# Retention attention and a top-2 expert layer: queries in 1-KB rows, later weight loads, and five expert tiles inside the last routing

## The chip, the cores and the metric

The kernel runs on one core of one Trainium2 chip. The metric is the device time of one execution in microseconds; the comparison is between the medians of repeated executions of the kernel before and the kernel after. Engines are named as in the profile: PE is TensorE's matmul, PEld its weight load, DVE VectorE, ACT ScalarE, POOL GpSimd, SP the queue that issues most DMAs.

## What is computed

```python
# q, k, v: (8 batches, 8 heads, 576 positions, 64)
scores = q @ k.T / 8
ret = scores * gamma[h] ** (i - j)     # where i >= j, else 0; gamma = 1 - 2**(-5-h)
x = (ret @ v)                          # as rows of 512: 4608 tokens (8 heads x 64)

logits = x @ w_gate + log1p(exp(x @ w_noise)) * noise       # 8 experts
top2, weights = two largest, softmax over the two
out = sum over the two experts e of  weight * (relu(x @ w1[e]) @ w2[e])   # 512 -> 1024 -> 512
```

## The kernel before, in words

**Attention.** Each batch's 576 positions are 512 plus a tail of 64. A *unit* is one batch and four heads (16 units); units 4b to 4b+3 make a pair of batches (`bp`), 1152 tokens. `Attention.load(u)` brings in a unit's q, k and v, two DMAs of 256 KB each per tensor: a partition holds two adjacent tokens of a head, so a row of a DMA is 2 x 64 x 4 = 512 bytes. `cast` makes bf16 copies: keys and values on POOL, queries on ACT. `tr` transposes queries or keys on PE, `scores` makes the scores of half a unit (mask on DVE), `states` the running sums of key times value (copied out on ACT), `out` the unit's output (decay on DVE, into `xT`). The `*_tail` functions do the 64-position tails of a pair.

**Routing.** `Router.route(bp)` is a Python generator that routes the 1152 tokens of a pair in 18 pieces. It computes the gate matmuls (L383), the logits `lg` (L388), the two best experts on DVE, the rank of each token in its expert's list with a matmul (L470, L472) over running counts `cum`, and writes the tokens with their gate values as rows of 1056 bytes to a DRAM table `xd` (L531). At the end a matmul of two one-hot tables (L551) adds the tokens' row numbers to the lists `L` (L555). `finish` turns `L` into the list of row numbers `xi` (three DVE instructions, L564 to L567), and `overflow_list` works out tiles for tokens beyond the lists' capacity (here there are none in the profile).

First choices (the lower-numbered expert of a token's two) fill an expert's list from the front, second choices from the back. Each list has 1280 slots, five tiles of 256 tokens.

**The order of work.** Rounds n = 0 to 16 of the main loop issue the parts of unit n and n-1. Seven times a round `step()` advances the pending routing by one piece. Under `manual_schedule` the order in which instructions are written is their order on each engine. A routing is put in the pending list near the end of rounds 4, 8, 12 and 16; the last one has no attention work beside it and runs out in `while pend: step()`. Weights of experts 0 and 1 are loaded by POOL-queue DMAs with a cast (L924, L927) after rounds 5, 7, 9 and 11.

**Experts.** `experts` loops over 40 tiles (8 experts x 5). For tile i: `gather` (an indirect DMA by `xi`, two halves of 128 rows), `transp` (8 transposes), `g1` (32 matmuls of 128x256, relu on ACT or DVE), `g2` (16 matmuls of 128x512). `g2` of a tile is interleaved with `g1` of the next. First choices' results go to a DRAM table `yd`; for second choices the first result is gathered back (`prev`), added (`comb`) and scattered to the output (`scat`). Weights of experts 2 to 7 are loaded through staging buffers and cast on ACT during the loop (`wload`, `wcast`). 11 DVE memsets (L717, L719) clear the gather buffers; they are outside the hand-written order.

Of the kernel before, what the change touches and what calls it, by code (L numbers as in the profile page):

```python
# [9 lines left out]
F32 = mybir.dt.float32  # L10
# [23 lines left out]
NOV = 80  # L34
# [4 lines left out]
CAPB = [P * (HPE - n) for n in ONLYA]  # L39
ROW0 = [P + sum(CAPA[:e]) for e in range(E + 1)]  # L40
# [5 lines left out]
def constants(nc, cp):  # L46
# [21 lines left out]
    for h in range(2):  # L68
        for rs in range(2):
            m = K["mask"][h * HD:(h + 1) * HD, rs, :].rearrange("p (r q) -> p r q", r=2)  # L70
            nc.gpsimd.affine_select(m, m, pattern=[[1, 2], [2, HD]], base=-rs, channel_multiplier=-2,
                                    compare_op=Alu.is_ge, fill=0.0)
# [8 lines left out]
    K["tok"] = cp.tile([P, 4, NC9], F32, name="tok")  # L81
    for h in range(2):
        t = K["tok"][h * HD:(h + 1) * HD]
        for b in range(2):
            nc.gpsimd.iota(t[:, :, 4 * b:4 * b + 4], pattern=[[1152, 4], [P, 4]], base=h + 576 * b,
                           channel_multiplier=2, allow_small_or_imprecise_dtypes=True)
# [13 lines left out]
def decay_tables(nc, cp, tmp):  # L100
# [5 lines left out]
    nc.gpsimd.iota(tv[:, :512].rearrange("p (c r q) -> p c r q", c=4, r=2), pattern=[[P, 4], [1, 2], [2, HD]],  # L106
# [20 lines left out]
class Attention:  # L127


    def __init__(self, tc, ctx, K, q, k, v):  # L130
# [5 lines left out]
        self.raw = ep("at_raw", 4)  # L136
# [21 lines left out]
    def load(self, u, queues):  # L158
        bp, hq, b = self.unit(u)
        d = self.u[u] = {}  # L160
        for n, q in zip("qkv", queues):
            r = self.raw.tile([P, 2, 4, P], F32, name=f"raw_{n}")
            for c in range(2):
                q.dma_start(out=r[:, c], in_=self.src[n][2 * bp + b, 4 * hq:4 * hq + 4, 256 * c:256 * c + 256, :].rearrange(  # L164
                    "h (p r) d -> p h (r d)", r=2))
            d["raw" + n] = r
# [9 lines left out]
    def cast(self, u):  # L176
# [6 lines left out]
        for r in range(2):  # L183
# [8 lines left out]
        qb = self.bf.tile([P, 2, 2, 4, HD], BF16, name="qb")  # L192
        nc.scalar.activation(qb.rearrange("p r c h d -> p (c h) r d"),
                             d.pop("rawq").rearrange("p c h (r d) -> p (c h) r d", r=2), Act.Copy, scale=0.125)
# [29 lines left out]
    def tr(self, u, n):  # L224
# [5 lines left out]
        for hp in range(2):  # L230
            for c in range(2):
                for r in range(2):
                    nc.tensor.transpose(p[:, hp, c, r, :], src[:, r, c, 2 * hp:2 * hp + 2, :].rearrange(
                        "p h d -> p (h d)"), self.K["ident"])
# [3 lines left out]
        d[n.upper()] = t  # L238

    def scores(self, u, hp):  # L240
# [3 lines left out]
        for c in range(2):  # L244
            for r in range(2):
                for h in range(2):
                    s = slice(h * HD, (h + 1) * HD)
                    for e in range(2):
                        nc.tensor.matmul(p[h][e * HD:(e + 1) * HD, c, r, :].rearrange("p (r q) -> p r q", r=2),  # L249
                                         lhsT=d["K"][s, hp, c, r, e, :], rhs=d["Q"][s, hp, c, :, e, :],  # L250
# [30 lines left out]
    def out(self, u):  # L281
# [17 lines left out]
        for e in range(2):  # L299
            for hp in range(2):  # L300
                for c in range(2):
                    j = 2 * c + e
                    if j:
                        nc.tensor.matmul(p[e][:, hp, c, :].rearrange("p (r q) -> p r q", r=2),
                                         lhsT=d["T", hp][:, j - 1, :], rhs=d["Q"][:, hp, c, :, e, :], start=False,
# [32 lines left out]

class Router:
# [13 lines left out]

    def load_noise(self, j):
# [3 lines left out]
        nq = nm[:, :512, :].rearrange("b (c q r) e -> q r b c e", q=HD, r=2)  # L358
        nt = nm[:, 512:, :].rearrange("(p b) s e -> s b p e", b=2)
        for c in range(4):  # L360
            nc.sync.dma_start(out=self.noise[j * HD:(j + 1) * HD, :, c, :], in_=nq[:, j, :, c, :])
        nc.sync.dma_start(out=self.noiset[j * HD:(j + 1) * HD], in_=nt[:, j])

    def route(self, bp):
# [112 lines left out]
        V.tensor_mul(pd, M, pr)  # L477
# [3 lines left out]
        V.tensor_copy(prs, pr[:, :, 0])  # L481
        V.tensor_add(prs, prs, pr[:, :, 1])
# [73 lines left out]
        else:  # L556
            V.tensor_copy(self.L, pT)

# [10 lines left out]
    def overflow_list(self):  # L569
# [4 lines left out]
        pn = self.at.ps.tile([P, 2, E], F32, name="R", bufs=1)  # L574
        nc.tensor.matmul(pn.rearrange("p a e -> p (a e)"), lhsT=self.K["ones"],
                         rhs=self.cum[:, NCOL].rearrange("p a e -> p (a e)"), start=True, stop=True)
# [3 lines left out]
        V.tensor_copy(ct, pn[:, 0])  # L580
        V.tensor_add(ct, ct, pn[:, 1])
# [484 lines left out]
```

## Time and profile before

| | |
|---|---|
| timed runs | 625.11, 619.98, 621.22 us; median 621.22 us |
| profiled execution | 616.24 us, of which the span in the trace is 614.7 us |
| mean granted TensorE clock | 0.821 of full speed |
| busy in the span | PE 460.4 us (75%), PEld 318.8 (52%), DVE 288.5 (47%), ACT 259.4 (42%), POOL 269.1 (44%) |
| moved by DMA | 104.19 MB, 170 GB/s on average |

The page cuts the span into 40 slices of 15.4 us. A digit is the busy share of a slice in tenths; the row PEclk gives the clock that TensorE was granted, in tenths. In rows of the order of time the first two numbers are start and duration in us, and a bracket at the end holds the idle time of the engine before that instruction with what ended it. "issue" is idle time in which the engine waited for nothing that the profile shows. A matmul's duration includes its passage through the array, so matmuls overlap: their spacing, not their duration, is the rate.

### The profile page before, as it was taken

To read this page: it belongs to the slowest core of one execution; us is meant where nothing else is said; L and a number is where in the kernel's file an instruction comes from. 1 tells how busy PE (TensorE), PEld (TensorE's weight loads), DVE (VectorE), ACT (ScalarE), POOL (GpSimd) and SP (SyncE) were. 2 spreads that over 40 slices of the span, in tenths; PEclk is the share of its full clock that TensorE was granted. 3 is DMA by queue.
4 is the path that set the end of the run, shared out by engine and by line. 5 is a ranking of instruction groups with operands and counts; after the bars stand their busy time and mean duration, and the time that the engine had idled before them with its cause. 6 is when DMAs were issued, how large, how long until landed. Compare 5 with 4: busy or idle time off the path is not lost.

```text
span 614.7 us, 11772 instructions
## 1 busy us (share of the span) xinstructions
PE 460.4 (75%) x4625; PEld 318.8 (52%) x4625; DVE 288.5 (47%) x783; ACT 259.4 (42%) x366; POOL 269.1 (44%) x339
## 2 busy tenths in 40 slices
PE   0688648828746334699999799899799598899960
PEld 0466536627634223466667356566466365565640
DVE  0266896798788775133333134234143243344440
ACT  6557625724641311165465154364354351332200
POOL 9644544337031037621303702705616447656560
PEclk9987557656676555889999979989989799989995
DMA  9997999969102322265666645665765554434450
GB/s 224 270 245 173 227 283 268 251 126 225 29 2 81 136 80 76 79 188 190 190 216 208 204 158 197 208 207 173 232 201 189 199 166 132 152 119 132 135 185 24
DMA packets 104491, 104.19 MB, mean 170 GB/s; under 512 B 25575, under 2 KB 81385, under 8 KB 104432
## 3 DMA queue, kind: packets, MB, share of 16 engines
q1 hardware_dynamic: 87088, 69.51, 39.3%
q0 software_dynamic: 15232, 32.84, 19.9%
q10 hardware_dynamic: 2112, 1.05, 0.7%
q8 instruction: 37, 0.61, 0.4%
q14 instruction: 22, 0.18, 0.1%
HBM read 84.66 MB, written 28.72 MB: 184 GB/s over the span
## 4 chain that ended last, share of the span: by engine, by line
PE 30%; issue 25%; DVE 19%; POOL 7%; DMA 6%; ACT 4%; SPq 4%; another core or an unknown queue 2%; POOLq 0%; ACTq 0%; DVEq 0%
PE p L807 11%; PE po L826 10%; POOL xg L758 4%; DVE S L254 3%; PE T L270 2%; SPq L164 2%; DVE olo L535 2%; SPq L172 2%; PE R L551 2%; DVE xT L310 2%; POOL prv L834 2%; DMA xg<-xd,xi 1%; DMA prv<-yd,ix 1%; POOL out_dram L868 1%
## 5 line engine op out<-in xcount | busy, mean ns | idle before, releaser
L807 PE MATMUL p<-xgT,w 128*128 128x256 bf16 x1280 | 254.4, 283 | 20.9 <-issue 20.3
L826 PE MATMUL po<-w,hT 128*128 128x512 bf16 x640 | 249.0, 393 | 6.7 <-issue 4.4
L807 PEld LDWEIGHTS <-w 128*128 128x128 bf16 x1280 | 129.1, 101 | 115.9 <-issue 40.0
L814 DVE TENSOR_SCALAR hT<-p 128x512 bf16<-128x512 f32 x80 | 55.2, 691 | 224.9 <-PE p L807 150.8
L812 ACT ACTIVATE hT<-p 128x512 bf16<-128x512 f32 x80 | 47.8, 597 | 198.8 <-PE p L807 91.4
L758 POOL DMA_INDIRECT xg<-xd,xi x80 | 81.4, 1018 | 44.3 <-issue 21.4
L868 POOL DMA_INDIRECT out_dram<-o,ix x45 | 45.6, 1014 | 124.5 <-DVE o L862 116.9
L826 PEld LDWEIGHTS <-hT 128*128 128x128 bf16 x640 | 64.2, 100 | 19.9 <-issue 10.2
L834 POOL DMA_INDIRECT prv<-yd,ix x45 | 45.6, 1014 | 32.3 <-DMA wst<-in_moe_w_dram 18.9
L254 DVE TENSOR_TENSOR S<-S,mask 128x512 bf16<-128x512 f32 x64 | 41.1, 684 | 37.5 <-PE S L249 37.5
L794 ACT ACTIVATE xgT<-pt 128x1024 bf16<-128x1024 bf16 x40 | 40.8, 1019 | 21.3 <-PE pt L791 18.3
L754 ACT ACTIVATE w<-wst 128x1024 bf16<-128x1024 f32 x48 | 47.9, 1048 | 0.0
L437 POOL TENSOR_TENSOR cum<-cum,M 128x16 bf16<-128x16 bf16 x36 | 8.0, 222 | 64.8 <-DVE d L442 62.3
L791 PE MATMUL pt<-ident,xg 128*128 128x128 bf16 x320 | 27.0, 225 | 12.5 <-issue 4.6
L276 ACT ACTIVATE Tb<-T 64x512 bf16<-64x512 f32 x32 | 18.9, 589 | 39.8 <-PE T L270 39.4
L184 POOL TENSOR_SCALAR_AFFINE_SELECT kn<-raw_k 128x512 bf16<-128x512 f32 x32 | 24.5, 789 | 24.5 <-DMA raw_k<-in_k_dram 16.3
L862 DVE SCALAR_TENSOR_TENSOR o<-po,g,prv 128x512 f32<-128x512 f32 x45 | 31.7, 743 | 2.9 <-DMA prv<-yd,ix 1.7
L189 POOL TENSOR_TENSOR vn<-raw_v,vg 128x1024 bf16<-128x1024 f32 x16 | 30.9, 1934 | 3.7 <-DMA raw_v<-in_v_dram 3.5
L791 PEld LDWEIGHTS <-xg 128*128 128x128 bf16 x320 | 21.9, 100 | 15.6 <-DMA xg<-xd,xi 9.2
L378 ACT ACTIVATE xr<-tr 128x512 bf16<-128x512 bf16 x36 | 20.8, 596 | 20.2 <-PE tr L377 17.6
L320 PE MATMUL S<-TT 64*128 64x128 bf16 x32 | 7.0, 235 | 29.4 <-DVE S L254 17.5
L249 PE MATMUL S<-QT,KT 64*64 64x128 bf16 x512 | 18.9, 274 | 12.3 <-DVE S L254 10.9
(183 smaller groups left out, 560.2 us busy)
## 6 DMA issues: line engine op xcount, KB each, us to landing
wst<-in_moe_w_dram SPq DMA_DIRECT2D x48, 512.0 KB
yd<-y SPq DMA_DIRECT2D x21, 512.0 KB
raw_k<-in_k_dram SPq DMA_DIRECT2D x32, 256.0 KB
raw_v<-in_v_dram SPq DMA_DIRECT2D x32, 256.0 KB
raw_q<-in_q_dram SPq DMA_DIRECT2D x28, 256.0 KB
xd<-xr SPq DMA_DIRECT2D x12, 396.0 KB
w<-in_moe_w_dram POOLq DMA_DIRECT2D x4, 1024.0 KB
xg<-xd,xi POOLq DMA_INDIRECT x80
```

Source lines behind the costliest of these rows:

```text
L254: nc.vector.tensor_tensor(S, p[h], self.K["mask"].unsqueeze(1).to_broadcast([P, 2, 2, P]), Alu.mult)
L754: nc.scalar.activation(W[e][:, k * F:(k + 1) * F], t, Act.Copy)
L758: nc.gpsimd.indirect_dma_start(out=xgs[i % NX][:, s, :], out_offset=None, in_=xd[:, :], in_offset=IOff(ap=keep["xi"][:, 2 * i + s:2 * i + ...
L791: nc.tensor.transpose(pt[:, di, s * P:(s + 1) * P], xb[:, di * P:(di + 1) * P], K["ident"])
L794: return lambda: nc.scalar.activation(xgT, pt, Act.Copy)
L807: nc.tensor.matmul(p1[:, f2, :], lhsT=w[:, o:o + P], rhs=xgT[:, di, :], start=(di == 0), stop=(di == KD - 1))
L812: nc.scalar.activation(hT[:, 2 * fp:2 * fp + 2, :], p1, Act.Relu)
L814: V.tensor_relu(hT[:, 2 * fp:2 * fp + 2, :], p1)
L826: nc.tensor.matmul(po[s], lhsT=hT[:, fi, s * P:(s + 1) * P], rhs=w[:, o:o + DM], start=(fi == 0), stop=(fi == KF - 1))
L834: nc.gpsimd.indirect_dma_start(out=prv[i % NP][:, s, :], out_offset=None, in_=yd[:rows, :], in_offset=IOff(ap=st[i]["ix"][:, s, 1:2], axis=0),
L862: V.scalar_tensor_tensor(o[:, s, :], st[i]["po"][s], st[i]["g"][:, s:s + 1], prv[i % NP][:, s, :], Alu.mult, Alu.add)
L868: ins = nc.gpsimd.indirect_dma_start(out=out[:, :], out_offset=IOff(ap=st[i]["ix"][:, s, 0:1], axis=0), in_=st[i]["o"][:, s, :], in_offset ...
```

## The change

*Queries.* A partition now holds four adjacent tokens of a head, so the 512 positions are loaded by one DMA of 512 KB per unit with rows of 1024 bytes. The casts, the transposes' output order, the masks, the decay table, the token numbers and the noise loads follow the new order of positions; a noise load of 64 partitions becomes two of 32.

*Weight loads.* The four loads of experts 0 and 1 move from after rounds 5, 7, 9, 11 to after rounds 11, 12, 13, 14.

*Early tiles.* Five tiles of first choices, three of expert 0 and two of expert 1, are computed by a generator `early` between the steps of the last routing. It starts when three pairs are routed: once after round 15, then one piece after each `step()` of round 16 and of the last `while pend` loop, and whatever is left after `overflow_list`. Its buffers are the query, key and value buffers of finished units. For this `route` now calls `finish` after the pairs 1 and 2, and a table `fill` raises the ranks of later tokens if an early tile had fewer tokens than slots. The expert loop runs over the other 35 tiles (`LATE`), whose first three gathers use query buffers too; the raw-input pool stays open for that. Weights of experts 2 to 7 are spread over the loop by a new table `loads`.

```diff
+EARLY = [(2, 0, 0), (2, 0, 1), (2, 1, 0), (3, 0, 2), (3, 1, 1)]     # pairs needed, expert, tile
+LATE = [(e, t) for e in range(E) for t in range(NTE) if (e, t) not in [x[1:] for x in EARLY]]
...
     # Attention.load
+            if n == "q":
+                q.dma_start(out=r.rearrange("p c h w -> p (c h w)").rearrange("p (h w) -> p h w", h=4),
+                            in_=self.src[n][2 * bp + b, 4 * hq:4 * hq + 4, :512, :].rearrange(
+                                "h (p r) d -> p h (r d)", r=4))
+                continue
...
+def early(tc, K, at, keep, xd, yd, W, tiles, routed):
+    nc = tc.nc
+    st = []
+    def gather(i):
+        if len(st) > i + 2 or len(st) == len(tiles) or tiles[len(st)][0] > len(routed):
+            return
+        n, e, t = tiles[len(st)]
+        raw = lambda s: at.raw.tile([P, 2, 4, P], F32, name="raw_" + s).rearrange("p c h w -> p (c h w)")
+        xg = raw("q")[:, :2 * XW].rearrange("p (s w) -> p s w", s=2)
+        nc.gpsimd.memset(xg, 0.0)
+        rows = n * NC9 * P
+        for s in range(2):
+            j = e * HPE + 2 * t + s
+            nc.gpsimd.indirect_dma_start(out=xg[:, s, :], out_offset=None, in_=xd[:rows, :],
+                                         in_offset=IOff(ap=keep["xi"][:, j:j + 1], axis=0),
+                                         bounds_check=rows - 1, oob_is_err=False)
...
+    def transp(i):      # 8 transposes into a "tr" buffer of PSUM, copied out on ACT
+    def g1(i, fp):      # 8 matmuls of 128x256 into an "S" buffer, relu on ACT
+    def g2(i, s):       # 8 matmuls of 128x512 into an "x" buffer, scaled on ACT; after s = 1 a DMA to yd
...
+    for _ in range(3):
+        gather(0)
+    yield
+    transp(0)
+    yield
+    for i in range(len(tiles)):
+        for fp in range(KF // 2):
+            g1(i, fp)
+            gather(i)
+            yield
+        for s in range(2):
+            if not s and i + 1 < len(tiles):
+                while len(st) == i + 1:
+                    yield
+                    gather(i)
+                transp(i + 1)
+                yield
+            g2(i, s)
+            gather(i)
+            yield
...
     # Router.load_noise
-        for c in range(4):
-            nc.sync.dma_start(out=self.noise[j * HD:(j + 1) * HD, :, c, :], in_=nq[:, j, :, c, :])
+        for r in (2 * j, 2 * j + 1):
+            for c in range(4):
+                nc.sync.dma_start(out=self.noise[r * 32:r * 32 + 32, :, c, :], in_=nq[:, r, :, c, :])
...
     # Router.route
-        V.tensor_mul(pd, M, pr)
+        prf = sp.tile(SH, F32, name="prf", bufs=1)
+        V.tensor_tensor(prf, pr, self.fill.unsqueeze(1).to_broadcast(SH), Alu.add)
+        V.tensor_mul(pd, M, prf)
...
-        V.tensor_copy(prs, pr[:, :, 0])
-        V.tensor_add(prs, prs, pr[:, :, 1])
+        V.tensor_add(prs, prf[:, :, 0], prf[:, :, 1])
...
+        if bp + 1 in self.atleast:          # pairs 1 and 2
+            self.finish()
+            pn = self.counts(bp + 1)        # one matmul of ones with the running counts
+            least = self.atleast[bp + 1]
+            V.tensor_sub(least, least, pn)
+            V.tensor_tensor(self.fill, self.fill, least, Alu.max)
+            yield
...
     # experts
+        loads = {}
+        i0 = -4
+        for e in range(2, E):
+            i0 = max(i0 + 4, LATE.index((e - 3, NTE - 1)) + 1 if e > 2 else 0)
+            for j in range(4):
+                loads[i0 + j] = e, j
...
     # main program
-        zero = at.cp.tile([P, DM], F32, name="zero")
-        nc.gpsimd.memset(zero, 0.0)
-        nc.sync.dma_start(out=yd[:P, :], in_=zero)
+        nc.sync.dma_start(out=yd[:P, :], in_=at.Tb[3].rearrange("p a b c -> p (a b c)").bitcast(F32))
...
+        def step():
+            while pend and next(pend[0], pend) is pend:
+                pend.pop(0)
+                routed.append(0)
+                if len(routed) == 3:
+                    work.append(early(tc, K, at, keep, xd, yd, W, EARLY, routed))
+            if n == NU:
+                more()                      # one piece of early
...
-            if n in (5, 7, 9, 11):
-                load_weights(nc, wp, moe_w1, moe_w2, (n - 5) // 4, W, (n - 5) // 2 % 2)
+            if n in (11, 12, 13, 14):
+                load_weights(nc, wp, moe_w1, moe_w2, (n - 11) // 2, W, (n - 11) % 2)
+            if n == NU - 1:
+                more()
         while pend:
             step()
         rt.finish()
+        for i in range(3):
+            xg = raw.tile([P, 2, 4, P], F32, name="raw_q").rearrange("p c h w -> p (c h w)")[:, :2 * XW].rearrange(
+                "p (s w) -> p s w", s=2)
+            nc.gpsimd.memset(xg, 0.0)
+            for s in range(2):
+                gather(tc, keep, xd, xg, i, s)
+            pre.append(xg)
         rt.overflow_list()
+        while work:
+            more()
```

More of the change, by code (lines that the diff above doesn't have):

```diff
@@ L352, in __init__ @@
         self.moe_noise = moe_noise
+        self.fill = self.one.tile([P, 2, E], F32, name="fill")
+        nc.vector.memset(self.fill, 0.0)
+        self.atleast = {}
+        for n in (2, 3):
+            t = self.atleast[n] = self.one.tile([P, 2, E], F32, name=f"atleast{n}")
+            nc.vector.memset(t, 0.0)
+            for e in range(E):
+                k = sum(x[0] <= n and x[1] == e for x in EARLY)
+                if k:
+                    nc.vector.memset(t[:, 0, e:e + 1], float(k * TS))
     def load_noise(self, j):
@@ L749, in wcast @@
                 return
-            e = i // NTE + 2
+            e = loads[i][0]
             if e not in W:
@@ L970, with more @@
         rt = Router(tc, actx, K, at, wgn, moe_noise, xd, keep)
[L971 to L973 removed]
+        nc.sync.dma_start(out=yd[:P, :], in_=at.Tb[3].rearrange("p a b c -> p (a b c)").bitcast(F32))
         NU = 16
         pend = []
[L977 to L980 removed]
+        routed = []
+        work = []
+        def more():
+            while work and next(work[0], work) is work:
+                work.pop(0)
+        def step():
[6 more added lines that the diff above has]
+                more()
         at.cast(0)
```

158 lines of the change are left out of this document (101 added, 57 removed).

## The prediction

> **What bounds the kernel now.** I read the page first: its slices say where each engine is busy, and the line under them which clock TensorE was granted.
>
> ```profile
> span 614.7 us, 11772 instructions
> PE   0688648828746334699999799899799598899960
> DVE  0266896798788775133333134234143243344440
> PEclk9987557656676555889999979989989799989995
> PE 30%; issue 25%; DVE 19%; POOL 7%; DMA 6%; ACT 4%; SPq 4%; another core or an unknown queue 2%; POOLq 0%; ACTq 0%; DVEq 0%
> ```
>
> A slice is 15.4 us. In the first 13 (to 200 us, attention and three routings) PE and DVE share the load; in the next three PE falls to 6, 3, 3 while DVE works at 8, 7, 7; then PE is at 9 or more for 23 slices (the expert loop) with DVE at 3. PE and its "issue" time are over half of the chain that ended last. So there are three stages with three limits, and the middle one leaves PE idle. The windows view puts numbers on it (busy us and instruction count of PE, PEld, DVE, ACT, POOL; then granted clock, DMA share, GB/s):
>
> ```profile
> 160.00:170.00 10.00, 8.31 (x155) 6.71 (x156) 7.29 (x24) 7.44 (x12) 0.65 (x3) 0.68 0.01 2
> 190.00:200.00 10.00, 7.83 (x170) 5.95 (x169) 8.45 (x16) 2.11 (x4) 0.00 (x0) 0.81 0.19 61
> 200.00:220.00 20.00, 6.68 (x82) 5.20 (x80) 15.75 (x68) 8.29 (x14) 2.14 (x9) 0.51 0.29 105
> 220.00:240.00 20.00, 4.55 (x31) 3.56 (x31) 13.83 (x42) 1.02 (x1) 10.28 (x9) 0.50 0.28 89
> ```
>
> From 200 to 240 PE works 11.2 of 40 us, at half clock. That hole is where the change puts five tiles. Its events come from the order of time:
>
> ```profile
> 196.22 1.00 PE L296 MATMUL x<-S,vn 64*64 64x128 bf16 x30
> 196.67 0.32 DVE L555 TENSOR_TENSOR L<-L,R 128x160 f32<-128x160 f32 x1
> 200.55 1.12 PE L383 MATMUL R<-wgn,xT 128*128 128x16 bf16 x36
> 201.40 0.50 DVE L717 MEMSET xg<- 128x528 f32 x1 [0.35 <-DVE xT L335]
> 201.82 0.24 DVE L388 COPY lg<-R 128x144 f32<-128x144 f32 x1
> 204.61 1.07 PE L377 MATMUL tr<-ident,xT 128*128 128x128 bf16 x8 [2.07 <-ACT xr L378]
> 207.65 0.91 DVE L719 MEMSET prv<- 128x1024 f32 x1 [0.16 <-issue]
> 213.34 0.28 PE L470 MATMUL R<-M,ltri 128*128 128x144 bf16 x1 [6.88 <-DVE M L432]
> 227.88 2.56 PE L551 MATMUL R<-oh,olo 128*128 128x160 bf16 x18 [9.46 <-DVE oh L545]
> 230.48 0.32 DVE L555 TENSOR_TENSOR L<-L,R 128x160 f32<-128x160 f32 x1 [2.65 <-PE R L551]
> 231.22 0.24 DVE L567 SCALAR_TENSOR_TENSOR xi<-xrow,z 128x80 int32<-128x80 f32 x1
> 232.32 1.14 POOL L758 DMA_INDIRECT xg<-xd,xi  x1 [6.64 <-DVE nti L585]
> 233.77 1.04 POOL L758 DMA_INDIRECT xg<-xd,xi  x1 [0.31 <-issue]
> 235.34 0.61 PE L791 MATMUL pt<-ident,xg 128*128 128x128 bf16 x4 [4.30 <-DVE cmp L598]
> 241.11 4.12 PE L807 MATMUL p<-xgT,w 128*128 128x256 bf16 x19
> 590.98 3.62 PE L826 MATMUL po<-w,hT 128*128 128x512 bf16 x16
> L794 ACT ACTIVATE xgT<-pt 128x1024 bf16<-128x1024 bf16 x40 | 40.8, 1019 | 21.3 <-PE pt L791 18.3
> ```
>
> The last attention unit's output starts at 196.2; the last routing's logits reach DVE at 201.8; its list of rows, xi, is complete at 231.5; the first expert matmul is at 241.1 and the last ends at 594.6. (The last row is a group of the page.) Between 201.8 and 231.5 PE waits for DVE (6.88 and 9.46 us in one piece).
>
> **Part 1, fewer tiles in the loop.** 40 tiles take 594.6 - 241.1 = 353.5 us, 8.84 each. Undisturbed stretches are quicker, stalled ones slower (L826 alone, 16 matmuls a tile):
>
> ```profile
> 300.00:330.00 30.00, 23.93 (x64) 1.00 0.61 199
> 330.00:360.00 30.00, 17.53 (x42) 0.85 0.59 190
> 480.00:510.00 30.00, 18.11 (x46) 0.89 0.55 180
> ```
>
> 64 matmuls are four tiles: 7.5 us each. The other two hold 2.6 and 2.9, with PE gaps that the trace calls issue. Such stretches are spread over the loop, so five tiles take their share: 5 x 8.84 = **-44** us; if the stalls go by time and not by tile, 5 x 7.5 = -37.5. Weights of expert 2 must now be ready after 5 tiles instead of 10; they are still loaded and cast one tile ahead, two transfers a tile at a mean DMA share near 0.6, so 0.
>
> **Part 2, five tiles in the hole.** The order in which the steps are written is the order on each engine. The early work starts at the end of round 15, needs xi of three routings, and goes one step per routing step: 1 for transposing tile 0, then 4 + 1 + 2 per tile (four first-GEMM steps, transposing the next, two second-GEMM steps), 35 after the gathers. Round 16 has 7 step calls and 18 follow until the last routing ends, so 25 run inside it and 10 behind it.
>
> *A new wait.* Route 2's L555 ends at 197.0; the three instructions that make xi end 0.65 us later on DVE (the same three follow L555 at the end by that much), 197.7. From gather issue to PE takes 3.0 us (232.32 to 235.34), the second half is issued 1.45 later and its four transposes cost 0.6: tile 0 is transposed at about 202.7. That transpose stands on PE ahead of out(15), which started at 196.2 (the states of unit 15 are late by some 2 us as well, behind the new count matmul that waits for L555, and hide under this). Behind it wait out(15), the tail scores, the gate matmuls, and so DVE's whole last routing: **+6.5**.
>
> *PE work before the logits.* Four first-GEMM steps are 32 matmuls; cold they go at 4.12/19 = 0.22 us, 1.7 for the first eight, then 0.9 a step: 4.4; transposing tile 1 0.6; one second-GEMM step between the halves of the gate matmuls 1.7: **+6.7**. Logits at 201.8 + 13.2 = 215.0.
>
> *The routing chain.* 29.6 us from logits to xi, DVE at 0.75 of it. PE's early steps before the rank matmul (L470) come to 1.7 + 4 x 0.9 + 0.6 and five row transposes of 1.07/2: 8.6, less than the 11.5 us that DVE needs to get there, hidden. From there to L551 they are 12 to 13 us against DVE's 11.5, and two steps lie between the halves of L551: +2 net of a faster clock. xi at 246.6. If PE is never late: 0; if each of the three PE steps on the chain waits a full second-GEMM step: +5.
>
> *Behind it.* 10 steps: 5 x 0.9 + 4 x 1.7 + 0.6 = 11.9, and under them the gathers of the next tiles (1.45 us apart, 3.0 to land) and DVE's overflow list, which cover each other. Third, the next gather buffer is one that early tile 3 still holds, for about 5 us; two other tiles' gathers take as long. Then two transposes and their ACT copy, 2.2 (1.0 for the copy): first loop matmul at about 260.7. PE still waits several us for DVE before L470, so part of the stretch runs at half clock: **+2.5** (0 to 25, below). 263 against 241.1: **+22**, between +17 (no lateness on the chain, full clock) and +47.
>
> **Part 3, queries and weights.** The loads:
>
> ```profile
> 15.54 1.82 SPq L164 DMA_DIRECT2D raw_q<-in_q_dram  x2
> 23.63 1.27 POOL L184 TENSOR_SCALAR_AFFINE_SELECT kn<-raw_k 128x512 bf16<-128x512 f32 x2 [4.44 <-DMA raw_k<-in_k_dram]
> 42.05 4.56 SPq L361 DMA_DIRECT2D noise<-in_moe_noise_dram  x4
> 52.95 1.06 ACT L193 ACTIVATE qb<-raw_q 128x1024 bf16<-128x1024 f32 x1 [1.33 <-DMA raw_q<-in_q_dram]
> 56.85 1.90 POOL L189 TENSOR_TENSOR vn<-raw_v,vg 128x1024 bf16<-128x1024 f32 x1 [0.79 <-DMA raw_v<-in_v_dram]
> 147.07 0.93 POOL L927 DMA_DIRECT2D w<-in_moe_w_dram  x1
> 184.82 2.68 POOL L529 COPY xr<-pl 128x24 f32<-128x24 f32 x3 [10.02 <-DVE pl L526]
> 30.00:40.00 10.00, 8.28 (x180) 6.32 (x174) 7.77 (x16) 6.82 (x8) 5.96 (x6) 1.00 1.10 241
> 266.00:270.00 4.00, 4.00 (x30) 2.65 (x28) 0.69 (x1) 1.71 (x3) 0.00 (x0) 1.00 0.90 292
> ```
>
> One query DMA in place of two saves about 0.9 us of SP's queue per unit, and before unit 2's keys at 23.6 (4.44 us late, with POOL's next casts and the tail transposes behind them) stand one such DMA and 1.6 MB of queries. 512-byte rows move 241/1.10 = 219 GB/s at full share, the loop's 4-KB rows 292/0.90 = 324. For 1-KB rows I take the nearer end, a sixth more: 1.0 us of 7.2, with SP's 0.9 and a little later **-2.5** (0 to -6). The Trainium skill ("DMA: Bandwidth & Descriptors", Specifications) gives 512 bytes as the smallest transfer at line rate; by that the rows bring only the issue time and the sum is 1.0 us worse. The two rows above differ by half and so speak against it, though they differ in more than row length.
>
> Noise: 8 transfers of half the size for 4, twice, on SP ahead of units 6 and 7: between 0 and 4.6 us each time; the ACT wait at 53 shows little slack: **+1**. The extra count in route 1 makes PE wait for L555 once on the chain: +1.5 (0 to 3). The five small DVE instructions that it adds to routes 1 and 2 are in that. Copy, add and multiply around the ranks stay three. POOL's iotas (10 for 6) end before PE asks for the first keys: 0.
>
> Weights: they leave 71 to 148 us, where no engine waits for input after 57, so 0 there; they land in 148 to 197, where DMA is idle (share 0.01 at 160). The last is queued on POOL behind xr, 187.5, its half expert is first needed by tile 2, after 220. If they lay in the way of route 2's row writes, tile 0's gather would be 1 to 2 us later. Part 3 together: **0** (-5 to +5).
>
> **Sum.** 0 + 22 - 44 = -22: span 593, the execution 594 against its 616.2. The median shown, 621.2, is 5 above that execution, so **599** is what I expect to be timed.
>
> **Rivals.** *Half clock (other side).* 18 matmuls went in 4 us at clock 0.57, 30 at 1.00:
>
> ```profile
> 262.00:266.00 4.00, 4.00 (x18) 2.16 (x16) 1.43 (x5) 3.21 (x5) 1.48 (x2) 0.57 0.49 155
> ```
>
> Early tiles at that rate are 12.5 us, +25: 602 + 22 = 624, no change; at 0.50 they are 15, +37 and 636. It decides at a mean clock of 0.63 over the stretch (even), 0.57 (1% slower). For: 0.50 in this hole now. Against: 0.81 at 190 to 200 with PE busy 0.78, which the stretch will be. Slower 0.08, even 0.05. The Trainium skill ("TensorE: Matmul & The Clock Gate", HAM oscillation) says idle gaps over about 3.4 us bring the half rate back; the waits above would be such gaps, and more than two of them in the stretch would lead here. The trace agrees so far: 0.50 after a 6.88 us gap.
> *Hidden better.* DVE's 11 memsets (7 x 0.50 + 4 x 0.91 = 7.1 us, inside the last routing from 201.4) fall into the new waits, and the queries' gain is at its end: -32, 589. For: DVE now idles 6 us longer before the logits. 0.15.
> *Stalls go by time:* 37.5 saved, 606. For: from 300 to 330 there is none, while 480 to 510 loses more than a quarter. 0.14.
> *Not what it says:* were an early tile short of tokens, slots would be filled up and others pushed to the overflow loop. The inputs give 539 and 484 first choices of experts 0 and 1 over two pairs of batches, 796 and 749 over three, against 512, 256, 768 and 512 needed: none. 0.01.
>
> Forecast (591 to 605): 0.57. Range 585 to 613: it leaves out the slower rival and a little more. One per cent, 6 us, is about what a measurement tells from no change: faster 0.85, within 0.07, slower 0.08.
>
> **What would show it.** PE's transposes of tile 0 at 202 to 203 with out(15) behind; logits near 215, xi near 247; the loop's first matmul at 258 to 268; 8.5 to 9 us a tile after it; a clock of 0.7 or more from 205 to 255. Wrong if the clock stays near 0.5, if xi comes after 255, or if loop tiles get slower because expert 2's weights come late.

## The result, and the profile after

| | before | after |
|---|---|---|
| median of repeated executions | 622.53 us (619.98 to 625.11) | 601.43 us (598.49 to 604.54) |
| profiled execution, and its span | 616.24, 614.7 us | 599.09, 597.5 us |
| mean granted clock | 0.821 | 0.847 |

The ratio is 0.9662 (95% interval 0.9586 to 0.9738): 3.4% faster, against a forecast of 599 us. (The median of before includes the runs taken beside the kernel after.) The page of the kernel after, with three of the rows shown of before:

```profile
span 597.5 us, 11717 instructions
...
PE   0687738828756678968998799799798798989960
...
PEclk9989758655875697988999699799799698999995
```

A slice is now 14.9 us. In slices 14 to 17, between the third routing and the loop, PE stood at 3, 3, 4, 6 (the prediction's 6, 3, 3 begin one slice earlier); it now stands at 6, 7, 8, 9, and its clock there is no longer 5. The windows view of the same stretch:

```profile
196.20:206.50 10.30, 6.64 (x65) 4.94 (x66) 1.29 (x2) 2.94 (x5) 8.57 (x10) 0.50 0.29 82
...
200.00:220.00 20.00, 18.88 (x204) 14.08 (x206) 9.41 (x25) 11.26 (x19) 6.64 (x8) 0.84 0.22 68
220.00:240.00 20.00, 14.00 (x93) 8.54 (x93) 16.82 (x59) 10.28 (x17) 9.08 (x16) 0.83 0.29 101
...
224.00:231.00 7.00, 4.66 (x17) 2.10 (x17) 6.12 (x37) 2.67 (x5) 4.37 (x12) 0.54 0.14 40
```

PE works 32.9 us from 200 to 240 instead of 11.2, at a clock of 0.84 and 0.83 instead of 0.5. The events in the order of time (L662 is the list L555 of before, L688 is xi, L494 the logits, L576 the rank matmul; L384, L393 and L403 are an early tile's transposes, first and second GEMM; L926, L942 and L961 those of the loop):

```profile
194.34 0.31 DVE L662 TENSOR_TENSOR L<-L,R 128x160 f32<-128x160 f32 x1
...
196.19 1.11 POOL L371 DMA_INDIRECT raw_q<-xd,xi  x1 [10.44 <-DVE fill L670]
...
199.23 0.59 PE L384 MATMUL tr<-ident,raw_q 128*128 128x128 bf16 x4 [3.17 <-POOL raw_q L367]
...
200.44 0.61 PE L384 MATMUL tr<-ident,raw_q 128*128 128x128 bf16 x4 [0.63 <-DMA raw_q<-xd,xi]
...
200.98 1.07 PE L312 MATMUL x<-S,vn 64*64 64x128 bf16 x32
...
213.43 0.27 DVE L494 COPY lg<-R 128x144 f32<-128x144 f32 x1
...
223.84 0.28 PE L576 MATMUL R<-M,ltri 128*128 128x144 bf16 x1 [3.61 <-DVE M L538]
...
243.14 0.24 DVE L688 SCALAR_TENSOR_TENSOR xi<-xrow,z 128x80 int32<-128x80 f32 x1
...
261.37 5.20 PE L942 MATMUL p<-xgT,w 128*128 128x256 bf16 x32
...
573.75 3.62 PE L961 MATMUL po<-w,hT 128*128 128x512 bf16 x15
```

Between the same marks of the two first traces (a list's mark is the start of its row here and below): route 2's list comes 2.3 us earlier (194.34 against 196.67), from there to the first loop matmul it takes 67.0 us instead of 44.4 (+22.6), the loop 316.0 instead of 353.5 (-37.5). The sum, -17.2, is the difference of the spans. The medians differ by 21.1 because the profiled execution of before was 6.3 us below its median and that of after only 2.3 below.

The start of the loop holds a wait that was not there before, on the third buffer that the gathers ahead of the loop ask for (L1185 clears it, L823 gathers):

```profile
261.61 1.02 ACT L929 ACTIVATE xgT<-pt 128x1024 bf16<-128x1024 bf16 x1 [0.86 <-PE pt L926]
...
262.89 0.55 POOL L1185 MEMSET raw_q<- 128x528 f32 x1
...
264.92 1.00 POOL L823 DMA_INDIRECT raw_q<-xd,xi  x1 [0.30 <-issue]
...
267.83 0.38 PE L926 MATMUL pt<-ident,raw_q 128*128 128x128 bf16 x4 [1.26 <-DMA raw_q<-xd,xi]
...
275.05 1.02 ACT L929 ACTIVATE xgT<-pt 128x1024 bf16<-128x1024 bf16 x1
```

The copies of transposed tiles on ACT (L929; those of the loop's second and third tile are shown) give each tile's time: the second tile takes the 13.4 us between these two, an undisturbed tile 7.4. (The expectations below call this the second tile behind the first.)

### The profile page after: what moved, and what is told of

The parts are those of the page before. It is cut to its first block, busy times and chain, and to the rows that moved or that the text cites. A ratio compares the mean times of both kernels' runs of the same rounds, so it can differ in the third digit from the quotient of the medians.

```text
span 597.5 us, 11717 instructions
## 1 busy us (share of the span) xinstructions
PE 454.6 (76%) x4587; PEld 315.4 (53%) x4627; DVE 277.8 (46%) x770; ACT 268.2 (45%) x381; POOL 274.3 (46%) x350
## 4 chain that ended last, share of the span: by engine, by line
PE 25%; issue 17%; POOL 5%; DMA 3%; DVE 2%; another core or an unknown queue 1%; POOLq 0%; ACT 0%; DVEq 0%; ACTq 0%
PE p L942 13%; PE po L961 11%; POOL xg L823 3%; DMA xg<-xd,xi 2%; PE pt L926 1%; POOL out_dram L1003 1%; POOL prv L969 1%; DVE o L997 1%; DMA raw_q<-xd,xi 0%; DMA out_dram<-o,ix 0%; DVE hT L949 0%; ACT xgT L929 0%; POOLq L823 0%; ACT hT L947 0%
## 5 line engine op out<-in xcount | busy, mean ns | idle before, releaser
L942 PE MATMUL p<-xgT,w 128*128 128x256 bf16 x1120 | 223.7, 283 | 18.2 <-issue 13.4
L961 PE MATMUL po<-w,hT 128*128 128x512 bf16 x525 | 205.3, 395 | 11.2 <-issue 9.7
L942 PEld LDWEIGHTS <-w 128*128 128x128 bf16 x1120 | 112.8, 101 | 98.8 <-issue 31.8
L949 DVE TENSOR_SCALAR hT<-p 128x512 bf16<-128x512 f32 x70 | 48.3, 691 | 195.3 <-PE p L942 106.0
L947 ACT ACTIVATE hT<-p 128x512 bf16<-128x512 f32 x70 | 41.8, 597 | 173.6 <-remote 62.9
L823 POOL DMA_INDIRECT xg<-xd,xi x64 | 66.0, 1032 | 19.2 <-issue 18.6
L961 PEld LDWEIGHTS <-hT 128*128 128x128 bf16 x560 | 56.3, 100 | 26.1 <-issue 17.4
L292 ACT ACTIVATE Tb<-T 64x512 bf16<-64x512 f32 x32 | 18.8, 589 | 44.7 <-PE T L286 44.4
L929 ACT ACTIVATE xgT<-pt 128x1024 bf16<-128x1024 bf16 x35 | 35.7, 1020 | 1.6 <-PE pt L926 1.6
L249 PE MATMUL tr<-ident,qb 128*128 128x128 bf16 x128 | 14.1, 277 | 21.4 <-ACT qb L203 16.3
L636 POOL COPY xr<-pl 128x24 f32<-128x24 f32 x12 | 12.1, 1048 | 28.1 <-issue 18.8
L251 ACT ACTIVATE QT<-tr 128x1024 bf16<-128x1024 bf16 x16 | 16.4, 1023 | 18.9 <-PE tr L249 18.9
```

What stands on the lines that cost most here:

```text
L823: tc.nc.gpsimd.indirect_dma_start(out=xg[:, s, :], out_offset=None, in_=xd[:, :], in_offset=IOff(ap=keep["xi"][:, j:j + 1], axis=0), bound ...
L929: return lambda: nc.scalar.activation(xgT, pt, Act.Copy)
L942: nc.tensor.matmul(p1[:, f2, :], lhsT=w[:, o:o + P], rhs=xgT[:, di, :], start=(di == 0), stop=(di == KD - 1))
L947: nc.scalar.activation(hT[:, 2 * fp:2 * fp + 2, :], p1, Act.Relu)
L949: V.tensor_relu(hT[:, 2 * fp:2 * fp + 2, :], p1)
L961: nc.tensor.matmul(po[s], lhsT=hT[:, fi, s * P:(s + 1) * P], rhs=w[:, o:o + DM], start=(fi == 0), stop=(fi == KF - 1))
```

## The experiments

Twelve kernels ran in three sets of four. The kernels of a set share a chip and the runs of before that they are compared with; the ratio is always to before in the same set. Before took 558.68 us in the first set, 619.22 in the second and 616.12 in the third, so times are compared within a set. Even ratios pass only between sets whose loops have stalls: the kernel after has 0.9662 in the first result and 0.9829 in set 1, where they are missing.

**Set 1: what the wait ahead of the loop and the first early steps cost.** `after_again` is the kernel after, unchanged.

> The changed kernel once more, beside the three variants of it. Expected 0.966 of the kernel before, within 0.960 to 0.972; it is the base that the variants are compared with. If the loop's stalls belong to places in the program and not to moments in time, they come again at the same tiles, near 327, 374, 419, 461 us.

Measured 549.42 us, 0.9829 (0.9797 to 0.986). Both parts missed. In this set's traces the loop has no stall: from the third to the last tile each takes 7.4 us, so the loop takes 268.0 us (260.19 to 528.16) instead of 316.0. The windows view (the columns of the prediction's) of 10 us in which the first trace of after has a stalled tile, then the same 10 us of this run:

```profile
326.00:336.00 10.00, 4.12 (x18) 1.75 (x19) 0.69 (x1) 0.69 (x2) 6.16 (x7) 0.67 0.58 175
```
```profile
326.00:336.00 10.00, 9.91 (x73) 6.90 (x74) 3.95 (x11) 6.28 (x10) 6.52 (x7) 1.00 0.95 314
```

18 matmuls against 73, with POOL as busy in one as in the other. In the stalled one PE's rows stand up to 1.4 us apart, behind nothing that the profile shows:

```profile
329.12 0.27 PE L942 MATMUL p<-xgT,w 128*128 128x256 bf16 x1 [1.27 <-issue]
329.61 0.37 PE L942 MATMUL p<-xgT,w 128*128 128x256 bf16 x1 [0.23 <-issue]
331.02 0.60 PE L961 MATMUL po<-w,hT 128*128 128x512 bf16 x1 [1.04 <-issue]
331.74 0.37 PE L942 MATMUL p<-xgT,w 128*128 128x256 bf16 x1
333.15 0.37 PE L942 MATMUL p<-xgT,w 128*128 128x256 bf16 x1 [1.03 <-issue]
```

`pre_k` moves the third gather ahead of the loop to a buffer of another set, which early tile 3 (counted from 0) doesn't hold:

```diff
-            xg = raw.tile([P, 2, 4, P], F32, name="raw_q")...
+            xg = raw.tile([P, 2, 4, P], F32, name="raw_q" if i < 2 else "raw_k")...
```

> The third tile of the loop is gathered into a key buffer in place of the query buffer that early tile 3 still holds. Theory: that held buffer pushes the clear and the gather behind ten other gathers on GpSimd (clear at 262.9, rows there at 269), and TensorE idles about 4 us between 266.6 and 271.4. Without it the clear comes before 252, the idle time goes, 3 to 5 us less than the changed kernel. Rival: TensorE would wait there anyway, for the first relus or at half clock; then within 1 us of the changed kernel.

Measured 539.84 us, 0.9657 (0.9626 to 0.9688), 9.6 us less than `after_again`, with intervals far apart. The last copy on ACT that reads early tile 3's buffer (L406), POOL's clearing of the buffer and PE's transposes of the new tile in it, in `after_again`; then the clearing and the transposes here:

```profile
250.29 0.69 ACT L406 ACTIVATE raw_v<-x,raw_q 128x512 f32<-128x512 f32 x1 [0.90 <-PE x L403]
...
260.19 3.66 PE L942 MATMUL p<-xgT,w 128*128 128x256 bf16 x32
...
264.04 0.56 POOL L1185 MEMSET raw_q<- 128x528 f32 x1
...
269.04 0.58 PE L926 MATMUL pt<-ident,raw_q 128*128 128x128 bf16 x4 [5.20 <-DMA raw_q<-xd,xi]
```
```profile
252.35 0.56 POOL L1185 MEMSET raw_k<- 128x528 f32 x1
...
260.33 3.66 PE L942 MATMUL p<-xgT,w 128*128 128x256 bf16 x32
...
263.83 0.61 PE L926 MATMUL pt<-ident,raw_k 128*128 128x128 bf16 x8
```

The loop starts at the same time and its second tile takes 6.2 us instead of 15.8: the choice of buffer is the whole gain, twice what was expected. The holder's release doesn't date the clearing, though. Early tile 3's last copy ends at 250.98, and POOL, idle for about 0.3 us at a time at most from there on, clears the buffer 13 us later, behind eight gathers of later tiles; in `pre_k` the clearing comes ahead of them. So the wait is a place in POOL's queue. What put those gathers first the traces don't show: the order as written has them behind.

`late1` puts the early work off by one step, so that none of it but the gathers is ahead of out(15); `late6` by six, so that only tile 0's transposes stand on PE ahead of the last gate matmuls:

```diff
             if n == NU:
-                more()
+                steps.append(0)
+                if len(steps) > 1:       # late6: > 6
+                    more()
```

> Early work starts one routing step later, so that tile 0's transpose stands behind out(15) on TensorE and not ahead of it. Theory: the wait for the first gather (196 to 201, 4.8 us before out(15)) is then covered by out(15), which starts near 197; the logits come 2 to 4 us sooner and the total is 1 to 3 us less. Rival: TensorE's work sets the end of the stretch and the missing step moves behind xi: the same time within 1 us.

> Early work starts six steps later, behind the attention's last matmuls, so the last routing's logits wait for no early tile. Theory: logits near 200 in place of 213.4, xi near 231 in place of 243.4, more early pieces behind xi (16 in place of 10, some 7 us more); the loop starts 3 to 7 us sooner than at 261. Rival: the pieces before the logits fill time in which TensorE has nothing else, and moved behind xi they cost what they took: loop start at 261 or later, same or up to 4 us slower than the changed kernel.

`late1` took 549.63 us, 0.984 (0.9809 to 0.987), the same as `after_again`; `late6` 540.21, 0.9661 (0.9633 to 0.9689). The logits of the last routing and the loop's first matmul, with xi in two of them, in `after_again`, `late1` and `late6` (L1188 of `late6` is L1185 of the others):

```profile
214.80 0.27 DVE L494 COPY lg<-R 128x144 f32<-128x144 f32 x1
...
244.51 0.24 DVE L688 SCALAR_TENSOR_TENSOR xi<-xrow,z 128x80 int32<-128x80 f32 x1
```
```profile
214.09 0.24 DVE L494 COPY lg<-R 128x144 f32<-128x144 f32 x1
...
261.31 3.66 PE L942 MATMUL p<-xgT,w 128*128 128x256 bf16 x32
```
```profile
205.42 0.31 DVE L494 COPY lg<-R 128x144 f32<-128x144 f32 x1 [0.18 <-PE R L489]
...
237.24 0.24 DVE L688 SCALAR_TENSOR_TENSOR xi<-xrow,z 128x80 int32<-128x80 f32 x1 [2.46 <-DMA raw_q<-xd,xi]
...
254.92 0.56 POOL L1188 MEMSET raw_q<- 128x528 f32 x1
...
258.78 1.05 PE L926 MATMUL pt<-ident,raw_q 128*128 128x128 bf16 x8 [3.35 <-DMA raw_q<-xd,xi]
...
259.62 5.55 PE L942 MATMUL p<-xgT,w 128*128 128x256 bf16 x32
```

In `late1` the rival was right: logits only 0.7 us sooner, the same time. With six steps put off, the logits come 9.4 us earlier than in `after_again` and xi 7.3, but the loop starts only 0.6 earlier (2.0 if counted from route 2's list, which comes 1.4 later in this trace). Most of it is the same PE work in another order. But a new wait stands there too: the second tile's buffer is cleared only at 254.92, and PE waits 3.35 us for its gather. The time that `late6` gains lies behind the loop's start, where its second tile takes 8.0 us instead of 15.8, nearly as in `pre_k`; neither its theory nor its rival had that.

**Set 2: the parts one by one.** `early_none` has `EARLY = []`, so 40 tiles in the loop, but keeps the three gathers ahead of it; `w_back` loads the weights after rounds 5, 7, 9 and 11 again; `q_back` loads queries and noise as before, with the masks and tables that go with that; `no_count` leaves out the count behind the routes of pairs 1 and 2 (`counts`, `tensor_sub`, the maximum), so `fill` stays 0, which with these inputs changes no rank.

```diff
-EARLY = [(2, 0, 0), (2, 0, 1), (2, 1, 0), (3, 0, 2), (3, 1, 1)]
+EARLY = []                              # early_none
...
-            if n in (11, 12, 13, 14):
+            if n in (5, 7, 9, 11):          # w_back, with the loads' numbers of before
...
-            pn = self.counts(bp + 1)        # no_count
-            least = self.atleast[bp + 1]
-            V.tensor_sub(least, least, pn)
-            V.tensor_tensor(self.fill, self.fill, least, Alu.max)
```

> No early tiles: queries in 1-KB rows, late weight loads, the loop over all 40 tiles with its first three gathers in query buffers; the lists are not finished after pairs 1 and 2. What is left of the change's gain is the attention's part. My sum gave that part 0 (-5 to +5), the trace of the changed kernel 2.3 us at the end of route 2 and 5.6 us at the end of route 1: expected 0.990 to 0.998 of the kernel before, last routing's logits near 197. Rival: the early tiles are the whole gain, 1.000 within 0.002.

> Weights of experts 0 and 1 loaded after rounds 5, 7, 9 and 11 again. I priced their move at 0: then the same as the changed kernel within 1 us, and the end of route 1 stays near 145. Rival: moving them is what made attention 5.6 us faster by then (transfers of 2 MB out of a stage with DMA at full share): 2 to 5 us slower, route 1 ends near 148 to 150.

> Queries in 512-byte rows by two transfers again, with the old order of positions, masks, tables and noise loads. By my sum the rows brought 2.5 us less 1 for the noise: 1 to 2 us slower than the changed kernel, most of it lost by 35 us. Rival: 512 bytes are at line rate already and only SP's queue gains: within 1 us. Second rival: the rows made the 5.6 us by the end of route 1: 4 to 6 us slower.

> The count of tokens after pairs 1 and 2 and the two instructions that turn it into fill are left out; fill stays zero, which it is for these inputs. Theory: the count's matmul makes TensorE wait for the list's sum (1.6 us, twice in the trace) ahead of the next unit: 1 to 3 us faster than the changed kernel, with route 2 ending 1 to 2 us sooner. Rival: what follows waits for the vector engine anyway: same within 1 us.

| | us | ratio (95%) | route 1's list | route 2's, behind it |
|---|---|---|---|---|
| early_none | 621.34 | 1.0016 (0.9981 to 1.0051) | 145.10 | 46.42 |
| w_back | 604.15 | 0.9742 (0.9678 to 0.9807) | 147.78 | 48.99 |
| q_back | 602.77 | 0.9728 (0.9668 to 0.9787) | 144.83 | 49.27 |
| no_count | 601.01 | 0.9653 (0.958 to 0.9727) | 145.89 | 46.87 |
| after (first result) | 601.43 | 0.9662 (0.9586 to 0.9738) | 145.09 | 49.25 |

Without early tiles the gain is gone, so it is theirs, and the rival of `early_none` was right. The kernel after did not run in this set, so the other three are set against its first result, and none leaves the intervals, which are about 4 us to either side: between theories of 1 to 3 us and rivals of none they decide nothing. The rival of `w_back` fits its numbers (route 1's list at 147.78), but `late6_kv` of set 3, whose program is that of after up to there, comes to this mark at 147.84, so one trace can't tell it either. The last column resolves one part: the traces of set 2 without the count take 46.4 and 46.9 us from route 1's list to route 2's, all others of this table 49.0 to 49.3. The count is 2.4 us there (`no_count` against after). (`early_none` has no count either, since it is made for the early tiles alone.)

**Set 3: the spread of before, and two better starts of the loop.** `before_again` is before, unchanged. `none_pre0` is `early_none` without the three gathers ahead of the loop (`range(0)` for `range(3)`); its expectation names the counts as kept, but like `early_none` it has none.

> The kernel before, unchanged, for its trace on the chip of these runs. Ratio 1.00 (0.995 to 1.005). Theory that the loop's stalls belong to places in the program and to the chip: if tiles of 12 us and over appear, they are the tiles 14, 19, 24, 28, 32 and 34 again, as in the first trace; on a chip without them every tile takes 7.4 us and the time is about 560 us. Rival, that stalls come at random moments: the count may be alike but the tiles differ. The end of the last routing (first trace 231.46 us) is expected at 229 to 232 us.

> The kernel after without early tiles and without the three gathers ahead of the loop, so 40 tiles in the loop with the loop's own buffers, as before: what is left of the change is the query rows, the moved weights and the counts. Prediction's Part 3 said 0 (-5 to +5): ratio 1.00. The theory after the runs so far (the run without early tiles had the last routing's end at 226.3 us against 231.5, and lost it at the start of the loop): ratio 0.990 to 0.996, the last routing ending some 5 us before that of the kernel before and the loop starting as much earlier.

`before_again` took 612.81 us, 0.9988 (0.9949 to 1.0026); `none_pre0` 616.12, 1.0035 (0.9995 to 1.0075). Routes 1 and 2, xi and the loop's first matmul in `before_again`:

```profile
145.69 0.31 DVE L555 TENSOR_TENSOR L<-L,R 128x160 f32<-128x160 f32 x1
...
192.03 0.31 DVE L555 TENSOR_TENSOR L<-L,R 128x160 f32<-128x160 f32 x1
...
226.81 0.24 DVE L567 SCALAR_TENSOR_TENSOR xi<-xrow,z 128x80 int32<-128x80 f32 x1
...
236.33 4.05 PE L807 MATMUL p<-xgT,w 128*128 128x256 bf16 x18
```

and in `none_pre0`:

```profile
144.95 0.31 DVE L662 TENSOR_TENSOR L<-L,R 128x160 f32<-128x160 f32 x1
...
191.47 0.31 DVE L662 TENSOR_TENSOR L<-L,R 128x160 f32<-128x160 f32 x1
...
226.25 0.24 DVE L688 SCALAR_TENSOR_TENSOR xi<-xrow,z 128x80 int32<-128x80 f32 x1
...
236.99 5.34 PE L942 MATMUL p<-xgT,w 128*128 128x256 bf16 x32
```

The theory behind the second expectation fell. The 5 us by which variants seemed to be ahead of before at the last routing are in a second trace of before as well (xi at 226.81 against 231.22 in the first; its end, at 227.05, is outside the 229 to 232 expected): the first trace was late, by 5 us at route 1's list already. Query rows and moved weights together are worth nothing that these runs resolve.

Stalled tiles (12 us and over) behind the loop's start are 13, 18, 23, 27, 31 and 33 in the first trace of before, counted from 0 (the expectation counts from 1), and 8, 13, 18, 22, 26 and 29 in that of after, where tile i is tile i + 5 of before: the first five are the same tiles of the lists, the sixth is one off. `before_again` has 13, 18, 23, 27 and 32. So the stalls keep to places of the program, nearly to the tile, and not to the time since the loop's start, which differs by 40 us between the first pair.

`pre_k_b` is `pre_k` on this set's chip; `late6_kv` is `late6` with the three gathers ahead of the loop in one buffer each of the query, key and value sets.

```diff
+            xg = raw.tile([P, 2, 4, P], F32, name="raw_" + "qkv"[i])...     # late6_kv
```

> The kernel after with the third gather ahead of the loop in a buffer of the keys' set, repeated on the chip of these runs. Theory: the held buffer cost the kernel after about 6 us in the first profile (its second loop tile came 13.4 us behind the first, against 7.4 for an undisturbed one), so the second tile comes 6 to 8 us behind the first and the time is about 0.957 of before (0.953 to 0.962) on a chip with stalls, 0.966 on one without. Rival (the stalls are only put elsewhere): 0.966 on a chip with stalls too.

> Early tiles begin six steps later and the three gathers ahead of the loop take one buffer each of the queries', the keys' and the values' sets, all let go by early tile 1. Theory (the buffer of early tile 3 held the third gather): no wait for buffers is left, the first loop matmul comes at 255 to 258 us instead of 261, the first tiles are 6 to 8 us apart, and the time is 0.950 to 0.960 of before on a chip with stalls in the loop and 0.955 to 0.962 on one without. Rival (the start of the loop is bound by PE's own work or by the gathers' trips): no better than the run with the keys' buffer alone (within 0.3%).

`pre_k_b` took 594.49 us, 0.9659 (0.9599 to 0.9719); `late6_kv` 595.93, 0.9652 (0.9571 to 0.9733). In the trace of `pre_k_b` the second tile takes 8.7 us, against 13.4 in after (6 to 8 were expected), but the ratio is the 0.966 that its rival named: with stalls in the loop, whose sizes vary from run to run, 4.7 us are not resolved. In `late6_kv` the three gathers follow one another on POOL without a wait for a buffer, and still the loop starts no earlier:

```profile
239.48 0.24 DVE L688 SCALAR_TENSOR_TENSOR xi<-xrow,z 128x80 int32<-128x80 f32 x1 [2.26 <-DMA raw_q<-xd,xi]
...
263.13 0.86 PE L926 MATMUL pt<-ident,raw_q 128*128 128x128 bf16 x8 [3.49 <-ACT raw_v L406]
...
265.96 5.71 PE L942 MATMUL p<-xgT,w 128*128 128x256 bf16 x32
```

xi comes 5.5 us before that of `pre_k_b` (244.94), the loop 2.9 later (263.07 there). The rival's forecast was right, no better than `pre_k_b`; its reason is shown in part only. PE works 18.9 of the 26.2 us between xi's end and the loop and idles 7.3, the longest 3.49 us behind a copy on ACT that is itself late for a reason that the trace doesn't name. The version that beats both kernels is `pre_k` (`late6` is level with it), in the set without stalls by 1.7% of before's time against the kernel after; with stalls the two are level.

## Why the prediction was right, and where its steps were off

The forecast of -22 us came out at -21 by the medians, and its mechanism held: five tiles leave the loop, fill most of the hole, and push the last routing back by part of their time. That the two numbers meet within 1 us is luck. The loop gave 6.5 us less than forecast, Part 2 took 0.6 more, and 6.3 came back from two places that have nothing to do with the change: the first trace of before, late in its attention (2.3; against the second, route 2's list of after is 2.3 late), and the profiled executions' distances to their medians (4.0).

It also held only where the loop has stalls. In set 1 the same two kernels differ by 9.3 us, less than half of the forecast, and `pre_k` gains 18.8 there: without stalls the badly placed buffer shows in full. Where before is quicker in that set is not shown, since no trace of it was taken there.

*Part 1 (-44, alternative -37.5): mis-sized.* The loop saved 37.5 us in the first pair of traces, and 35.7 against `before_again` (236.33 to 588.00 there, 351.7 us). The step that failed is "five tiles take their share" of the stalls. The five removed tiles come from the first two experts, and the stalls behind the loop's start come later, five or six times in both kernels. The row PE of before had it: from slice 18 to 38 it isn't at 9 throughout, as the prediction reads it, but at 5 to 8 in six slices (23, 26, 29, 32, 34 and 35), where the six stalled tiles lie. So the tiles were worth about what an undisturbed tile takes, 7.4 us or 37. The value of the rival "stalls go by time" was right, its reason was not: they go by place.

*Part 2 (+22): the sum right, its chain in part.* Measured +22.6 from route 2's list to the loop, against the first trace of before, and +22.7 against the second. The pieces:

| | predicted | measured, counted from route 2's list |
|---|---|---|
| out(15) behind tile 0's transposes | +6.5 | 200.98 - 194.34 = 6.6, before -0.5: +7.1 |
| PE's early work before the logits | +6.7 | logits 19.1 behind the list, before 5.15: +13.9 with the wait, so +6.8 |
| routing chain, logits to xi | +2 | 29.95 against 29.64: +0.3 |
| xi to the first loop matmul | 16.6 (11.9 + 2.2 + 2.5) | 18.0 |

Each was near, but `late1` and `late6` show that the first two don't carry through to the end: with the logits 1.5 and 10.8 us closer to the list than in `after_again`, the loop starts 0.4 us later and 2.0 us sooner. What stays is PE's own work. From route 2's list to the loop's first matmul, before, then after (the columns as above):

```profile
196.67:241.11 44.44, 13.17 (x141) 10.05 (x141) 32.12 (x117) 10.26 (x17) 13.22 (x19) 0.54 0.27 91
```
```profile
194.34:261.37 67.03, 52.16 (x468) 35.87 (x473) 35.59 (x125) 32.88 (x52) 33.00 (x40) 0.87 0.40 128
```

PE works 39.0 us more; 16.4 of them went into time in which it had been idle, and 22.6 made the stretch longer. In each of the ten traces with early tiles this work is 50 to 53 us and the idle time 11 to 17, so what PE doesn't do ahead of the logits it does behind xi. I had summed a chain of waits; the larger part of the stretch is the engine's work. That no order of it starts the loop sooner isn't shown: `late6` and `late6_kv` hold waits of over 3 us ahead of it.

The half clock of the rival came in pieces. PE's one gap of over 3.4 us that shows in the stretch behind 200 us (3.61, at the rank matmul) stands with a granted clock of 0.54 in the 7 us from 224; from 231 to 238 it was 1.00 again. A longer piece, 0.50 in the 10.3 us from 196.2, stands beside waits of 3.17 and 0.63 us. The Trainium skill ("TensorE: Matmul & The Clock Gate", HAM oscillation) has gaps over about 3.4 us bring the half rate back, and this row agrees. The longer piece has no such gap. Nor was the prediction's "0.50 after a 6.88 us gap" an instance: before stands at 0.50 from 203 to 206.5 already, ahead of that gap. The mean from 200 to 240 stayed at 0.83, far from the 0.63 at which that rival would have been even.

*The third gather buffer (0): wrong.* "Two other tiles' gathers take as long" was the step that failed. It took POOL's order to be the written one, with the clearing ready when early tile 3 lets go; on the queue eight gathers stand ahead of it (see `pre_k`), and the first loop tile is too short to hide that and the tile's own trip (264.92 to the transposes at 267.83). It cost 9.6 us in the set without stalls. In the first trace the second loop tile takes 4.7 us more than in `pre_k_b`. In the total of the first pair it doesn't show, since before loses time at that place as well: in its first trace three tiles take 13.0, 11.0 and 7.8 us there, 9.6 more than 7.4 each; in the trace of after 13.4, 7.6 and 7.4, 6.2 more.

*Part 3 (0): right as a sum of rows and weights, not by its pieces.* The rows were put at -2.5 and the weights at 0; `none_pre0`, with both, is 1.0035 (0.9995 to 1.0075) of before, and `q_back` reaches route 1's list at 144.83, the kernel after at 145.09. The doubtful step is "a sixth more" bandwidth from 1-KB rows, taken from two rows of the trace that differ in more than row length: no run shows it, though ten traces with the same program up to that list put it at 144.95 to 147.84, so that 2.5 us are not ruled out either. The rule of the Trainium skill that I weighed against it ("DMA: Bandwidth & Descriptors", Specifications: 512 bytes are enough for line rate) is compatible with these runs. The count was put at +1.5 and took 2.4 on the chain from route 1 to route 2; SP's noise loads grew by 1.4 us in their first group (4.56 before), against the +1 that I took:

```profile
15.36 0.62 SPq L170 DMA_DIRECT2D raw_q<-in_q_dram  x1
...
40.26 5.93 SPq L467 DMA_DIRECT2D noise<-in_moe_noise_dram  x8
```

*From span to median.* I took the same 5 us between profiled execution and median for both kernels; it was 6.3 for before and 2.3 for after. By spans alone I would have been 4.5 us too low (593 against 597.5).

The rivals "slower by half clock" and "hidden better" did not come: the clock is shown above, and the logits came at 213.4, 11.6 us later than before, not earlier.

## What to carry to other kernels

When work is moved into an idle stretch, add up the engine's whole work from the last mark that doesn't move to the first that must follow, and set it beside the idle time there. A wait inside that stretch that ends sooner gains little while the engine has the same work to make up: here logits 9.4 us sooner brought the loop's start 0.6 to 2.0 us forward. Before pricing removed iterations at the loop's mean, list each iteration's time: where a few slow ones carry the stalls, ask whether the removed ones are among them. And price a borrowed buffer by where its clearing and its gather stand on the issuing engine's queue, and not only by when its holder lets go of it.

Take two traces of the kernel before if a part is worth a few microseconds: here two traces of the same program differ by 5 us at the end of route 1, more than any of the small parts.

## What the runs showed of the hardware that was not expected

The same two programs ran about 9% faster in the first set (558.68 against 616 to 622 us for before, 549.42 against 601.43 for after). The traces of after show where: the loop takes 268.0 us without stalls and 316.0 with them, while its first matmul comes at 260.19 and 261.37. In a stalled stretch PE's matmuls come up to 1.4 us apart with nothing shown that it waits for, the granted clock falls to 0.67 in the 10 us shown, and the places are nearly the same in every trace with stalls. What decides whether a run has them, the chip, its neighbours or something else, and what PE waits for stays open: no run here tells it apart. The record gives the number 15 for the chip of the first set, which has no stalls, and of the third, which has them and came 40 minutes later, and the number 5 for that of the second; if the number means one and the same chip, the chip alone doesn't decide it.
